# Attention stage re-planned: keys' maxima two pairs ahead, v copies shared with GpSimd, gate logits copied on VectorE, slots' rows scaled per head on ScalarE

## The chip, the cores and the metric

One core of one Trainium2 chip. The metric is the time of one execution in device microseconds; lower is better. The engines are named as in the profile: PE (TensorE matmul), PEld (its weight loads), DVE (VectorE), ACT (ScalarE), POOL (GpSimd) and SP (SyncE, which here only issues DMAs).

## What is computed

Three layers follow one another: attention without a sequence-by-sequence matrix, a top-1 mixture of experts, and a product of two projections.

```python
def _attn_ref(q, k, v):                      # 8 batches, 8 heads, 576 positions, 64 channels
    q_s = np.exp(q - np.max(q, axis=-1, keepdims=True)); q_s /= q_s.sum(-1, keepdims=True) + 1e-09
    k_s = np.exp(k - np.max(k, axis=2, keepdims=True));  k_s /= k_s.sum(2, keepdims=True) + 1e-09
    kv = np.einsum('bhsd,bhse->bhde', k_s, v)
    return np.einsum('bhsd,bhde->bhse', q_s, kv)
def _moe_ref(x, modality_id, w_gate, modality_bias, w1, w2):   # 4608 tokens, 8 experts, F = 1024
    logits = x @ w_gate + modality_bias[modality_id]
    e_idx = np.argmax(logits, axis=1)
    gate_w = softmax(logits)[arange, e_idx]
    for e in range(E):
        out[mask] = gate_w[mask] * (np.maximum(x[mask] @ w1[e], 0.0) @ w2[e])
def _moe2_ref(x, w1, w2, w3, w_out):
    return ((x @ w1) * (x @ w2)) @ w3 @ w_out
```

The keys' softmax runs over the positions, so its maximum is taken per channel over all 576 of them; the queries' softmax runs over the 64 channels of each head.

## The kernel before, in words

**Attention.** Two batches make a pair, so there are four pairs, c = 0 to 3. All large tiles exist twice (`z = c % 2`): `kt`, `qt`, `vt`. For each pair, `load` brings k, q and v in two DMAs each. `keys(c)` takes the maximum over positions: a tree of four `tensor_tensor` on DVE for each half of the heads (L303 to L306), four PE transposes into a PSUM bank (L312), a reduction on DVE (L315), eight small matmuls that spread the maxima over the partitions again (L320), a copy to `kr` on ACT (L323); then, for each of four groups g of two heads, three subtractions (L329, on DVE for c = 0, on GpSimd for the others) and one exponential on ACT (L330). `kvs(c)` copies v into `vp`, beside a column of ones (L341, ACT), multiplies (L348, PE), divides into `bd` on DVE (L355 to L357) and adds columns of gate logits to `bd` (L361 to L372), so that one product later gives the attention output, its sum and the gate logits. `queries(n)`, twelve of them, take three of a pair's nine position blocks each: maximum (L383) and subtraction (L384) on DVE into one of two tiles `qs`. `attend(c, j)`, nine per pair, transposes a block (L400, banks 6 and 7 in turn), takes exponentials on ACT (L403), multiplies by `bd` (L413) and copies the logits (L421) and the output (L422) from PSUM on ACT.

**Routing.** `route(c)` turns a pair's logits into expert, rank and gate. After the first two pairs (`BEARLY` = 4 batches) `early_table` and `early_lists` (L559 to L634) choose three expert slots of 512 tokens that can already be filled, with a final selection matmul on PE (L626, `pick`). The tile `ord` that comes of it holds the tokens' numbers and gates.

**Expert slots.** `slot(P, n)`: n = 0 to 2 are the early ones, six wide and one narrow slot follow. For each slot the rows of x are gathered by GpSimd's indirect DMA (L730, four tiles of 128 tokens), scaled on DVE by gate and sum (L736 to L738), transposed (L754), split into high and low parts on ACT and DVE (L758, L759), as are the weights (L701, L703), multiplied by w1 (L779), passed through ReLU and split (L765, L766), multiplied by w2 (L801) and copied out (L804). The experts' SBUF region lies over the attention's tiles: the first write there (`"Mb"`) waits until the last attend is over.

**Order.** Nothing is issued in the order of the text. Each step is added to a `Plan` with an engine, a cost, and what it reads and writes; `Plan.order` plays the steps through with these costs and puts on each engine the ready step with the lowest priority number (its number in the text plus `pri`). The engines then run that order in sequence, and each waits on semaphores for what it reads. So a changed cost or priority moves instructions on all engines. The first Plan covers attention, routing, slots 0 to 2 and the start of the next; a second one follows a branch (L927).

**The rest** (from about 600 us): the projections' weights are combined, then two stages of matrix products whose time is PE's.

Of the kernel before, what the change touches and what calls it, by code (L numbers as in the profile page):

```python
# [6 lines left out]
F32 = mybir.dt.float32  # L7
# [32 lines left out]
class Plan:  # L40
# [5 lines left out]
    def __init__(self, lat=0.12):  # L46
        self.lat = lat
        self.steps, self.last, self.readers = [], {}, {}

    def add(self, eng, cost, fn, r=(), w=(), pri=0.0, slack=0.0):  # L50
        i = len(self.steps)
        deps = set()
        for k in r:
            if k in self.last:
                deps.add(self.last[k])
            self.readers.setdefault(k, []).append(i)
        for k in w:
# [86 lines left out]
def body(tc, q, k, v, mod, wgate, mbias, w1, w2, m1, m2, w3, wo, out):  # L144
    nc = tc.nc
    V, G, SC, PE, SP = nc.vector, nc.gpsimd, nc.scalar, nc.tensor, nc.sync
    P = Plan()
    ctx = ExitStack()
# [145 lines left out]
    def keys(c):  # L294
# [26 lines left out]

        P.add("P", 1.8, to_rows, r=[K("cm", z)], w=[K("bk", 5)])
        P.add("S", ps_(512), lambda: SC.copy(r_.rearrange("p h d -> p (h d)"), bk), r=[K("bk", 5)], w=[K("kr", z)])  # L323
        for g in range(4):
            hs = slice(2 * g, 2 * g + 2)
            kg = [K("k", z, g)]
            en, e_, c_ = ("G", G, gt_(1152)) if c else ("V", V, vt_(1152))
            for js in (slice(3 * i, 3 * i + 3) for i in range(3)):
                P.add(en, c_ / 3 + 0.05, lambda hs=hs, e_=e_, js=js: e_.tensor_tensor(k_[:, hs, js], k_[:, hs, js], r_[:, hs].unsqueeze(2).to_broadcast([128, 2, 3, D]), op=ALU.subtract), r=[K("kr", z)], w=kg)  # L329
            P.add("S", sb_(1152), lambda hs=hs: SC.activation(k_[:, hs], k_[:, hs], AF.Exp), w=kg)  # L330

    def kvs(c):
# [6 lines left out]
        for g in range(4):  # L339
            w_ = vp[g % 2]  # L340
            P.add("S", sb_(1152), lambda g=g, w_=w_: SC.copy(w_[:, :, :, 0:64], v_[:, 2 * g : 2 * g + 2]), r=[K("v", z, g)], w=[K("vp", g % 2)])  # L341

            def mm(g=g, w_=w_):
                for j in range(NT):
                    for y in range(2):
                        for a in range(2):
                            p_ = slice(64 * y, 64 * y + 64)
                            PE.matmul(kv(y)[64 * a : 64 * a + 64, g], lhsT=k_[p_, 2 * g + a, j], rhs=w_[p_, a, j], start=(j == 0), stop=(j == NT - 1))  # L348

            P.add("P", 1.4, mm, r=[K("k", z, g), K("vp", g % 2)], w=[K("bk", 4), K("bk", 5)])  # L350
        for y in range(2):
# [18 lines left out]

            P.add("P", 0.9, gates, r=[K("kT", y), "wg"], w=[K("bk", 4 + y)])
            P.add("S", 0.2, lambda bk=bk, b_=b_: SC.copy(b_[:, :, 65:73], bk[:, 0:32].rearrange("p (c e) -> p c e", c=4)), r=[K("bk", 4 + y)], w=[K("bdg", n)])  # L372

    def queries(n):
# [6 lines left out]
        kq = [K("q", z, g) for g in range(4)]  # L381
        js = slice(3 * g, 3 * g + 3)
        P.add("V", vt_(1536), lambda: V.tensor_reduce(x[:, :, js], q_[:, :, js], axis=AX.X, op=ALU.max), r=kq, w=[K("qx", z, g)])  # L383
        P.add("V", vt_(1536), lambda: V.tensor_tensor(qs[(3 * c + g) % 2].rearrange("p j h d -> p h j d"), q_[:, :, js], x[:, :, js].unsqueeze(3).to_broadcast([128, H, 3, D]), op=ALU.subtract), r=kq + [K("qx", z, g)], w=[K("qs", (3 * c + g) % 2)])  # L384

    scattered, kept = [False], []

    def attend(c, j):
# [43 lines left out]

# [255 lines left out]
    def slot(P, n, after=(), parts="lsab", T=None, again=False):  # L688
# [16 lines left out]
        if "l" in parts:  # L705
# [26 lines left out]
            P.add("D", 5.9, lambda: wload("w2r", w2, "o (k p) f -> p (o k) f"), r=[rk_, "Ma"] + ([K("landed", xk) for _, _, xk in tiles] if n == 0 else []), w=[K("w2r", i) for i in range(8)], slack=2.0)  # L732
            for t, x_, xk in tiles:
                heads = x_.rearrange("p (h e) -> p h e", e=65)
                sums = heads[:, :, 64]
                P.add("V", 0.1, lambda sums=sums: V.tensor_scalar(sums, sums, 1e-9, None, op0=ALU.add), w=[xk], pri=-230)  # L736
                P.add("V", 0.12, lambda sums=sums: V.reciprocal(sums, sums), w=[xk], pri=-230)
                P.add("V", vt_(512), lambda t=t, heads=heads, x_=x_: V.scalar_tensor_tensor(out=x_[:, 0:512].rearrange("p (h e) -> p h e", e=64), in0=heads[:, :, 0:64], scalar=o[:, t, 1:2].bitcast(F32), in1=heads[:, :, 64:65].to_broadcast([128, H, D]), op0=ALU.mult, op1=ALU.mult), r=[ok], w=[xk], pri=-230)  # L738

# [582 lines left out]
```

## Time and profile before

| | us |
|---|---|
| median of 3 runs | 1216.51 (1213.94 to 1218.99) |
| profiled execution: time | 1220.7 |
| profiled execution: span from first to last instruction | 1219.0 |
| PE busy in the span | 1133.9 (93%) |
| DVE busy | 875.9 (72%) |
| ACT busy | 514.4 (42%) |
| POOL busy | 547.4 (45%) |

The span is what the views cut up; the 1.7 us between it and the execution's time lie around it. Times in the rows are us from the start of the span.

### The profile page before, as it was taken

The page shows a single profiled execution, that of the slowest core. Times are in us where ns is not written, and L with a number is a line of the kernel's source. Part 1 is how long each engine was busy: PE and PEld are TensorE (multiplying, and loading weights), DVE is VectorE, ACT ScalarE, POOL GpSimd, SP SyncE. Part 2 cuts the span into 40 slices and gives each one's busy share as a digit, 9 for nine tenths or more (in the row PEclk, how much of TensorE's full clock was granted, in tenths as well). Part 3 has the DMA queues.
Part 4 walks back from the last instruction along what each step waited for, and adds up shares of the span by engine and source line. Part 5 has one row for each costly group of instructions (what it writes and reads, how often), then busy time and mean ns, then how long its engine had stood idle before and what let it go on. Part 6 is the DMA issues. An engine that isn't in the chain of part 4 may idle for free.

```text
span 1219.0 us, 22861 instructions
## 1 busy us (share of the span) xinstructions
PE 1133.9 (93%) x8605; PEld 1033.1 (85%) x8605; DVE 875.9 (72%) x1483; ACT 514.4 (42%) x965; POOL 547.4 (45%) x536
## 2 busy tenths in 40 slices
PE   3677799899989999999999999999999999999996
PEld 3566677677878888888988999999999999999996
DVE  7878588888769989888645757576666689765550
ACT  3557564233334334334544332424242445655550
POOL 0355357843234344323133455555645576443332
PEclk9878789989999999999999999999999999999998
DMA  9982555654347566455644334444443348977741
GB/s 356 391 331 82 206 146 157 129 195 145 129 111 265 163 202 216 144 186 181 222 167 140 101 110 137 117 130 118 118 141 107 107 131 262 341 256 235 235 140 50
DMA packets 156139, 216.29 MB, mean 177 GB/s; under 512 B 19791, under 2 KB 90995, under 8 KB 156019
## 3 DMA queue, kind: packets, MB, share of 16 engines
q1 hardware_dynamic: 148946, 195.15, 49.9%
q0 software_dynamic: 7072, 19.60, 5.1%
q8 instruction: 69, 1.13, 0.4%
q14 instruction: 52, 0.42, 0.1%
HBM read 156.51 MB, written 74.97 MB: 190 GB/s over the span
## 4 chain that ended last, share of the span: by engine, by line
PE 68%; DVE 1%; DMA 1%; issue 1%; POOL 0%; ACT 0%; SPq 0%; DVEq 0%; POOLq 0%; ACTq 0%
PE pb L1134 29%; PE pb L1267 13%; PE pb L801 12%; PE pb L779 10%; PE pb L1025 3%; PE pb L754 1%; DMA ca<-p_dram 1%; PE pb L1012 1%; DMA p_dram<-ca 0%; DVE ar L1059 0%; DVE ar L999 0%; DVE ar L703 0%; POOL out_dram L1241 0%; DVE ca L1110 0%; SPq L1230 0%
## 5 line engine op out<-in xcount | busy, mean ns | idle before, releaser
L1134 PE MATMUL pb<-al,ar 128*128 128x384 f32 x1728 | 307.7, 335 | 1.1 <-ACT sx L1140 0.8
L1134 PEld LDWEIGHTS pb<-al,ar 128*128 128x128 f32 x1728 | 300.0, 188 | 1.6 <-ACT sx L1140 1.1
L801 PE MATMUL pb<-ar 128*128 128x512 f32 (+1 forms) x960 | 217.7, 385 | 0.0
L779 PE MATMUL pb<-ar 128*128 128x512 f32 (+1 forms) x960 | 216.0, 386 | 0.0
L779 PEld LDWEIGHTS pb<-ar 128*128 128x128 f32 x960 | 176.7, 192 | 35.2 <-DVE ar L759 0.4
L801 PEld LDWEIGHTS pb<-ar 128*128 128x128 f32 x960 | 175.2, 191 | 33.6
L1267 PE MATMUL pb<-ar 128*128 128x256 f32 x1512 | 182.9, 283 | 2.2 <-issue 1.3
L1267 PEld LDWEIGHTS pb<-ar 128*128 128x128 f32 x1512 | 181.8, 192 | 3.2 <-issue 1.3
L999 DVE TENSOR_TENSOR ar<-ca,ar 128x512 fp32r<-128x512 f32 x140 | 106.8, 770 | 55.2 <-ACT ar L998 43.7
L831 POOL TENSOR_TENSOR ca<-ca 128x512 f32<-128x512 f32 x40 | 57.3, 1437 | 107.4 <-DVE ca L830 98.4
L998 ACT CAST ar<-ca 128x512 fp32r<-128x512 f32 x140 | 86.2, 622 | 44.8 <-DMA ca<-p_dram 13.6
L765 ACT ACTIVATE ar<-pb 128x512 fp32r<-128x512 f32 (+1 forms) x80 | 46.1, 578 | 135.4 <-PE pb L779 118.2
L1140 ACT COPY sx<-pb 128x384 f32<-128x384 f32 x96 | 45.9, 481 | 90.8 <-PE pb L1134 60.9
L329 POOL TENSOR_TENSOR kt<-kt,kr 128x384 f32<-128x384 f32 x36 | 49.5, 1409 | 67.2 <-ACT kr L323 63.6
L1168 POOL TENSOR_TENSOR ca<-ca 128x384 f32<-128x384 f32 x48 | 54.1, 1128 | 52.1 <-DVE ca L1168 52.1
L804 ACT COPY yo<-pb 128x512 f32<-128x512 f32 (+1 forms) x40 | 22.6, 566 | 119.2 <-PE pb L801 115.3
L766 DVE SCALAR_TENSOR_TENSOR ar<-pb,ar 128x512 fp32r<-128x512 f32 (+1 forms) x80 | 52.4, 656 | 26.4 <-ACT ar L765 23.4
L703 DVE TENSOR_TENSOR ar<-w2r,ar 128x512 fp32r<-128x512 f32 x60 | 49.7, 862 | 21.2 <-ACT ar L701 20.6
L1143 POOL TENSOR_TENSOR ca<-ca,sx 128x384 f32<-128x384 f32 x24 | 29.4, 1224 | 77.7 <-ACT sx L1140 77.5
L1140 ACT COPY ca<-pb 128x384 f32<-128x384 f32 x48 | 22.9, 480 | 86.2 <-PE pb L1134 83.1
L1134 PE MATMUL pb<-thm,ar 128*128 128x384 f32 x288 | 58.2, 336 | 0.0
L730 POOL DMA_INDIRECT ca<-x_dram,ord x38 | 40.0, 1053 | 39.5 <-issue 13.0
(282 smaller groups left out, 1777.3 us busy)
## 6 DMA issues: line engine op xcount, KB each, us to landing
p_dram<-ca SPq DMA_DIRECT2D x168, 192.0 KB
ca<-p_dram SPq DMA_DIRECT2D x126, 256.0 KB
w1r<-in_moe_w_dram SPq DMA_DIRECT2D x10, 2048.0 KB
w2r<-in_moe_w_dram SPq DMA_DIRECT2D x10, 2048.0 KB
ca<-in_moe_w_dram SPq DMA_DIRECT2D x32, 512.0 KB
kt<-in_k_dram SPq DMA_DIRECT2D x8, 1152.0 KB
qt<-in_q_dram SPq DMA_DIRECT2D x8, 1152.0 KB
vt<-in_v_dram SPq DMA_DIRECT2D x8, 1152.0 KB
```

The lines of the kernel that those rows point to most:

```text
L329: P.add(en, c_ / 3 + 0.05, lambda hs=hs, e_=e_, js=js: e_.tensor_tensor(k_[:, hs, js], k_[:, hs, js], r_[:, hs].unsqueeze(2).to_broadcast( ...
L703: P.add(g, c, lambda: e.tensor_tensor(lo(), raw(), hi().bitcast(F32), op=ALU.subtract), r=[K(nm + "r", i), K(nm + "h", i), extra], w=[K(nm ...
L766: P.add("V", vt_(N), lambda hh=hh, hl=hl, p=p: V.scalar_tensor_tensor(out=hl(), in0=p(), scalar=0.0, in1=hh().bitcast(F32), op0=ALU.max, o ...
L779: PE.matmul(p(), lhsT=W1(i)[:, TURN[kk], ms], rhs=XT(z)[:, kk, cols], start=(kk == 0 and c == 0), stop=(kk == 3 and c == 2))
L801: PE.matmul(p(), lhsT=W2(i)[:, f, ns], rhs=HT(y)[:, f, cols], start=(f == 0 and c == 0), stop=(f == 7 and c == 2))
L831: P.add("G", gt_(512), lambda: G.tensor_tensor(Tf, Tf, Qf, op=ALU.add), r=[K("Q", b)], w=[K("T", b)])
L998: P.add("S", (ps_ if psum else sb_)(n), lambda: SC.copy(hi(), src), r=sk, w=[hk], pri=pri)
L999: P.add("V", vt_(n), lambda: V.tensor_tensor(lo(), src, hi().bitcast(F32), op=ALU.subtract), r=list(sk) + [hk], w=[lk], pri=pri)
L1134: PE.matmul(bk(j), lhsT=Mt[:, f, a, i, m, t], rhs=X(y, x)[:, t], start=(fresh and t == 0 and n == 0), stop=(t == 1 and n == 2), skip_group ...
L1140: P.add("S", ps_(HB), lambda j=j, to=to: SC.copy(S(to), bk(j)), r=[bkk(j)], w=[sk(to)])
L1168: P.add(eng, c(HB), lambda: e.tensor_tensor(t[:, sl], x, y, op=op), r=kk, w=[k_])
L1267: PE.matmul(bk(j), lhsT=At[z][:, m, i, f], rhs=Bt[:, x, y, f], start=(fresh and f == 0 and n == 0), stop=(f == 3 and n == 2), skip_group_c ...
```

## The change

It does these things:

- `keys(c)` is added two pairs ahead (`keys(1)` before the loop, `keys(c + 2)` after attend 8 of pair c), and uses the transposes' banks 7 and 6 in turn, where it used bank 5, which `kvs` uses too.
- Pair 0's subtractions go from DVE to GpSimd; of pair 1's twelve, four go from GpSimd to DVE (`SUBS_V`). Of the sixteen v copies, eight go to GpSimd (`VP`).
- The gate logits of each attend are copied from PSUM by DVE (`L2V`).
- Every kind of step gets a shift of its priority (`RANK`), several costs change, and the first Plan assumes 0.20 us between engines, not 0.12.
- From slot 1 on, sums and reciprocals are taken for two tiles at once, multiplied by the gate on DVE, and each head's 64 columns are scaled by an activation of their own on ACT, eight to a tile, where one DVE instruction did a tile.

```diff
+RANK = dict(load=-15, tree=-60, subs=-150, exps=15, kv=60, tail=-15, vp=-250, q=100, row=100)
+AFTER = (8, 8, 8)
+SUBS_V = (0, 1, 0, 0)
+VP = ("GSSG", "GSGG", "SSGG", "SSGS")
+L2V = 1
...
-    P = Plan()
+    P = Plan(0.2)
...
-        bk = bank[5]
+        qb = (7, 6)[rot("qb", 2)]
+        bk, bkk = bank[qb], K("bk", qb)
...
-            en, e_, c_ = ("G", G, gt_(1152)) if c else ("V", V, vt_(1152))
-            for js in (slice(3 * i, 3 * i + 3) for i in range(3)):
+            for i in range(3):
+                en, e_, c_ = ("V", V, 0.55) if i < SUBS_V[c] else ("G", G, 1.3)
+                js = slice(3 * i, 3 * i + 3)
...
-            P.add("S", sb_(1152), lambda g=g, w_=w_: SC.copy(w_[:, :, :, 0:64], v_[:, 2 * g : 2 * g + 2]), r=[K("v", z, g)], w=[K("vp", g % 2)])
+            P.shift = RANK["vp"]
+            en = VP[c][g]
+            e_, c_ = dict(S=(SC.copy, sb_(1152)), G=(G.tensor_copy, 1.35))[en]
...
-        P.add("S", 0.28, lambda: SC.copy(l_, pv[:, :, :, 64:73]), r=pk, w=[lk])
+        en, e_, c_ = ("V", V.tensor_copy, 0.2) if L2V else ("S", SC.copy, 0.28)
+        P.add(en, c_, lambda: e_(l_, pv[:, :, :, 64:73]), r=pk, w=[lk])
...
+                    if n == 0:
+                        P.add("V", vt_(512), lambda rows=rows, to=to, gate=gate: V.scalar_tensor_tensor(out=to, in0=rows[:, :, 0:D], scalar=gate, in1=rows[:, :, D : D + 1].to_broadcast([128, H, D]), op0=ALU.mult, op1=ALU.mult), r=[ok], w=[two[t]], pri=pri)
+                        continue
+                    P.add("V", 0.15, lambda rows=rows, gate=gate: V.tensor_scalar(rows[:, :, D], rows[:, :, D], gate, None, op0=ALU.mult), r=[ok], w=[two[t]], pri=pri)
+                    def scale(rows=rows, to=to):
+                        for i in range(H):
+                            SC.activation(to[:, i], rows[:, i, 0:D], AF.Copy, scale=rows[:, i, D : D + 1])
+                    P.add("S", 1.6, scale, w=[two[t]], pri=pri)
...
     kvs(0)
+    keys(1)
     biases()
     for c in range(4):
         load("k", c + 2)
-        keys(c + 1)
...
             attend(c, j)
+            if c < 2 and j == AFTER[c]:
+                keys(c + 2)
```

**On GpSimd**, all of the attention stage. `kt0` holds the keys of pairs 0 and 2, `kt1` those of pairs 1 and 3; before, one row stands for each of pairs 1, 2 and 3:

```order
L329 TENSOR_TENSOR kt1_116<-kt1_116,kr1_143 128x2x192 x12
L329 TENSOR_TENSOR kt0_115<-kt0_115,kr0_142 128x2x192 x12
L601 IOTA qt0_128 128x128
L329 TENSOR_TENSOR kt1_116<-kt1_116,kr1_143 128x2x192 x12
L730 DMA ca_94<-x_dram_59,ord_93 128x520 x5
```

and now (L341 are the subtractions, L358 the copies of v):

```order
L341 TENSOR_TENSOR kt0_115<-kt0_115,kr0_142 128x2x192 x7
L358 COPY vp1_139<-vt0_117 128x18x64
L341 TENSOR_TENSOR kt0_115<-kt0_115,kr0_142 128x2x192 x3
L341 TENSOR_TENSOR kt1_116<-kt1_116,kr1_143 128x2x192 x5
L358 COPY vp0_138<-vt1_118 128x18x64
L341 TENSOR_TENSOR kt1_116<-kt1_116,kr1_143 128x2x192 x3
L358 COPY vp0_138<-vt1_118 128x18x64
L358 COPY vp1_139<-vt1_118 128x18x64
L341 TENSOR_TENSOR kt0_115<-kt0_115,kr0_142 128x2x192 x12
L358 COPY vp0_138<-vt0_117 128x18x64
L341 TENSOR_TENSOR kt1_116<-kt1_116,kr1_143 128x2x192 x12
L756 DMA ca_94<-x_dram_59,ord_93 128x520 x4
```

Pair 0's twelve subtractions now stand first, eight of pair 1's follow, and the copies stand between them.

**On PE**, round the maxima of pair 3's keys (`mx1`, `cm1`) before. `bd0` and `bd1` at this place are pair 2's:

```order
L361 MATMUL pb4_75<-ident_84,bd0_150 64x128 x4
L361 MATMUL pb5_76<-ident_84,bd1_151 64x128 x4
L369 MATMUL pb4_75<-wg_156,kTs0_154 64x8 x8
L369 MATMUL pb5_76<-wg_156,kTs1_155 64x8 x8
L400 MATMUL pb7_78<-ident_84,qs1_133 128x128 x4
L312 MATMUL pb5_76<-ident_84,mx1_141 128x128 x4
...
L320 MATMUL pb5_76<-ident_84,cm1_145 64x128 x8
```

and now, where L365 with `kt0` is pair 2's kv product:

```order
L322 MATMUL pb6_77<-ident_84,mx1_141 128x128 x4
...
L365 MATMUL pb4_75<-vp0_138,kt0_115 64x65 x2
...
L330 MATMUL pb6_77<-ident_84,cm1_145 64x128 x8
...
L380 MATMUL pb4_75<-ident_84,bd0_150 64x128 x4
L380 MATMUL pb5_76<-ident_84,bd1_151 64x128 x4
```

Pair 3's maxima stood behind pair 2's finished kv product and its tail; they now stand inside that product.

**On ACT**, round the rows of slot 1 before (L758 splits a transposed block, L804 copies a result of slot 0 out):

```order
L701 CAST ar_2224<-w1r_1407 128x512 x3
L758 CAST ar_2224<-pb5_76 128x2x256
L804 COPY yo_2229<-pb3_2220 128x512
L758 CAST ar_2224<-pb7_78 128x2x256
```

and now:

```order
L776 ACTIVATE ca_94<-ca_94 128x64 x16
L844 COPY yo_2229<-pb3_2220 128x512
L798 CAST ar_2220<-pb5_76 128x2x256
L798 CAST ar_2220<-pb7_78 128x2x256
```

Sixteen activations, for two tiles of 128 tokens, stand ahead of the copy of slot 0's first result.

## Rows read from the trace of the kernel before

**Rows 1.** By stretch: busy PE, PEld, DVE, ACT, POOL; granted clock, DMA share, GB/s.

```profile
0.00:141.00 141.00, 90.61 (x2428) 77.92 (x2432) 110.47 (x193) 77.92 (x139) 52.12 (x52) 0.85 0.71 264
...
52.00:68.10 16.10, 7.01 (x186) 6.09 (x188) 16.03 (x17) 7.87 (x10) 16.10 (x12) 0.75 1.04 396
...
141.00:161.00 20.00, 15.28 (x324) 12.15 (x320) 7.29 (x19) 12.16 (x29) 4.91 (x5) 0.78 0.95 347
```

**Rows 2.** PE's waits from 0 to 161 us: total, times, longest.

```profile
PE pb L348 <- ACT kt L330: 24.9, 7, 5.1
```

**Rows 3.** Instructions in order of time, the chain of pair 3: start, duration.

```profile
114.04 15.98 POOL L329 TENSOR_TENSOR kt<-kt,kr 128x384 f32<-128x384 f32 x11
...
129.09 2.22 ACT L330 ACTIVATE kt<-kt 128x1152 f32<-128x1152 f32 x2 [3.15 <-POOL kt L329]
...
140.21 0.57 PEld L626 LDWEIGHTS <-qt 128*128 128x128 bf16 x18
...
161.02 14.23 PE L779 MATMUL pb<-ar 128*128 128x512 f32 x51
```

**Rows 4.** DVE's waits from 0 to 141 us: total, times, longest.

```profile
DVE rk L355 <- PE pb L348: 8.1, 4, 3.8
...
DVE ltri L249 <- POOL ltf L248: 2.1, 1, 2.1
DVE qx L383 <- DMA qt<-in_q_dram: 1.8, 1, 1.8
```

**Rows 5.** DVE's groups by line and shape, 0 to 141 us: busy, mean ns, idle before.

```profile
L384 DVE TENSOR_TENSOR qs<-qt,qx 128x1536 f32<-128x1536 f32 x12 | 22.5, 1879 | 5.2 <-PE pb L400 5.2
...
L303 DVE TENSOR_TENSOR tr<-kt 128x1024 f32<-128x1024 f32 x8 | 12.1, 1518 | 2.9 <-DMA kt<-in_k_dram 2.7
...
L329 DVE TENSOR_TENSOR kt<-kt,kr 128x384 f32<-128x384 f32 x12 | 5.7, 551 | 0.0
L621 DVE TENSOR_TENSOR qt<-qt 128x384 bf16<-128x384 f32 x6 | 5.4, 899 | 0.0
...
L569 DVE SCALAR_TENSOR_TENSOR t_tak<-t_tar,t_jE 128x3 f32<-128x3 f32 x1 | 1.0, 958 | 0.0
...
L470 DVE TENSOR_TENSOR ca<-pb,cnt 128x72 f32<-128x72 f32 x2 | 0.5, 225 | 0.0
```

**Rows 6.** Single DVE instructions in order of time, free of and beside GpSimd's work.

```profile
6.32 1.22 DVE L303 TENSOR_TENSOR tr<-kt 128x1024 f32<-128x1024 f32 x1 [2.71 <-DMA kt<-in_k_dram]
...
17.10 5.71 DVE L329 TENSOR_TENSOR kt<-kt,kr 128x384 f32<-128x384 f32 x12
...
22.73 1.75 DVE L384 TENSOR_TENSOR qs<-qt,qx 128x1536 f32<-128x1536 f32 x1
...
60.86 2.56 DVE L384 TENSOR_TENSOR qs<-qt,qx 128x1536 f32<-128x1536 f32 x1
```

**Rows 7.** GpSimd's groups by line and shape, 0 to 160 us, columns as in rows 5.

```profile
L329 POOL TENSOR_TENSOR kt<-kt,kr 128x384 f32<-128x384 f32 x36 | 49.5, 1409 | 67.2 <-ACT kr L323 63.6 <-PE pp L413 3.6
...
L261 POOL MEMSET zer<- 128x584 int32 x1 | 0.6, 611 | 0.0
```

**Rows 8.** GpSimd's subtractions of pair 1 alone: ns min/median/max, first and last start.

```profile
L329 POOL TENSOR_TENSOR kt<-kt,kr x12: 988/1182/2504, 51.8 to 66.1; 128x384 f32<-128x384 f32 x12
```

**Rows 9.** PE's waits from 160 to 330 us.

```profile
PE pb L465 <- DVE cnt L471: 4.6, 1, 4.6
...
PE pb L754 <- DVE ca L738: 1.9, 2, 1.4
```

**Rows 10.** One group of DVE from 161 to 345 us, columns as in rows 5.

```profile
L738 DVE SCALAR_TENSOR_TENSOR ca<-ca,ord 128x512 f32<-128x512 f32 x16 | 13.4, 836 | 0.0
```

**Rows 11.** ACT's groups by line and shape, 160 to 600 us, columns as in rows 5.

```profile
L701 ACT CAST ar<-w2r 128x512 fp32r<-128x512 f32 x80 | 49.2, 622 | 2.9
...
L457 ACT ACTIVATE ca<-ca 128x72 f32<-128x72 f32 x2 | 0.5, 264 | 2.9 <-DVE ca L456 2.9
```

**Rows 12.** One product of a wide slot in order of time.

```profile
317.46 21.92 PE L779 MATMUL pb<-ar 128*128 128x512 f32 x96
```

More of the change, by code (lines that the diff above doesn't have):

```diff
@@ L47, in __init__ @@
         self.lat = lat
-        self.steps, self.last, self.readers = [], {}, {}
+        self.steps, self.last, self.readers, self.shift = [], {}, {}, 0.0
     def add(self, eng, cost, fn, r=(), w=(), pri=0.0, slack=0.0):
@@ L63, in add @@
         deps.discard(i)
-        self.steps.append((eng, cost, fn, sorted(deps), i + pri, slack))
+        self.steps.append((eng, cost, fn, sorted(deps), i + pri + self.shift, slack))
     def order(self):
@@ L272, in load @@
             fn = lambda dst=dst, i=i: SP.dma_start(dst, src[2 * c + i].rearrange("(g y) (r j) d -> (y r) g (j d)", y=2, j=NT))
-            P.add("D", 3.7, fn, w=[K(n, z, g) for g in (2 * i, 2 * i + 1)], slack=1.0)
+            P.add("D", 3.05, fn, w=[K(n, z, g) for g in (2 * i, 2 * i + 1)], slack=1.0)
+        P.shift = 0.0
     def smalls():
@@ L300, in keys @@
         t2 = tr4[:, :, 0:2].rearrange("p h j d -> p h (j d)")
+        P.shift = RANK["tree"]
         for i in range(2):
@@ L312, in over_partitions @@
                 PE.transpose(bk[:, 128 * i : 128 * i + 128], xf[:, 128 * i : 128 * i + 128], ident)
-        P.add("P", 0.9, over_partitions, r=[K("mx", z)], w=[K("bk", 5)])
-        P.add("V", vt_(512), lambda: V.tensor_reduce(x_, bk.rearrange("p (c t) -> p c t", c=8), axis=AX.X, op=ALU.max), r=[K("bk", 5)], w=[K("cm", z)])
+        P.add("P", 0.6, over_partitions, r=[K("mx", z)], w=[bkk])
+        P.add("V", vt_(512), lambda: V.tensor_reduce(x_, bk.rearrange("p (c t) -> p c t", c=8), axis=AX.X, op=ALU.max), r=[bkk], w=[K("cm", z)])
         def to_rows():
@@ L320, in to_rows @@
                     PE.matmul(bk[64 * y : 64 * y + 64, 128 * i : 128 * i + 128], lhsT=x_[:, 2 * i + y : 2 * i + y + 1].to_broadcast([128, 64]), rhs=ident, start=True, stop=True)
-        P.add("P", 1.8, to_rows, r=[K("cm", z)], w=[K("bk", 5)])
-        P.add("S", ps_(512), lambda: SC.copy(r_.rearrange("p h d -> p (h d)"), bk), r=[K("bk", 5)], w=[K("kr", z)])
+        P.add("P", 0.75, to_rows, r=[K("cm", z)], w=[bkk])
+        P.add("S", ps_(512), lambda: SC.copy(r_.rearrange("p h d -> p (h d)"), bk), r=[bkk], w=[K("kr", z)])
         for g in range(4):
@@ L340, in kvs @@
             w_ = vp[g % 2]
[L341 removed]
+            P.shift = RANK["vp"]
+            en = VP[c][g]
+            e_, c_ = dict(S=(SC.copy, sb_(1152)), G=(G.tensor_copy, 1.35))[en]
+            P.add(en, c_, lambda g=g, w_=w_, e_=e_: e_(w_[:, :, :, 0:64], v_[:, 2 * g : 2 * g + 2]), r=[K("v", z, g)], w=[K("vp", g % 2)])
             def mm(g=g, w_=w_):
@@ L348, in mm @@
                             PE.matmul(kv(y)[64 * a : 64 * a + 64, g], lhsT=k_[p_, 2 * g + a, j], rhs=w_[p_, a, j], start=(j == 0), stop=(j == NT - 1))
-            P.add("P", 1.4, mm, r=[K("k", z, g), K("vp", g % 2)], w=[K("bk", 4), K("bk", 5)])
+            P.shift = RANK["kv"]
+            P.add("P", 1.1, mm, r=[K("k", z, g), K("vp", g % 2)], w=[K("bk", 4), K("bk", 5)])
+        P.shift = RANK["tail"]
         for y in range(2):
@@ L361, in tr @@
                     PE.transpose(bk[0:64, 128 * g : 128 * g + 128], b_[:, g, 0:64], ident)
-            P.add("P", 0.9, tr, r=[K("bd", n)], w=[K("bk", 4 + y)])
+            P.add("P", 0.7, tr, r=[K("bd", n)], w=[K("bk", 4 + y)])
             P.add("S", ps_(512), lambda bk=bk, T=T: SC.copy(T.rearrange("p c d -> p (c d)"), bk[0:64]), r=[K("bk", 4 + y)], w=[K("kT", y)])
@@ L369, in gates @@
                         PE.matmul(bk[64 * a : 64 * a + 64, 8 * g : 8 * g + 8], lhsT=T[:, g, 64 * a : 64 * a + 64], rhs=wg[:, 4 * (g % 2) + 2 * a + y], start=True, stop=True)
-            P.add("P", 0.9, gates, r=[K("kT", y), "wg"], w=[K("bk", 4 + y)])
+            P.add("P", 0.5, gates, r=[K("kT", y), "wg"], w=[K("bk", 4 + y)])
             P.add("S", 0.2, lambda bk=bk, b_=b_: SC.copy(b_[:, :, 65:73], bk[:, 0:32].rearrange("p (c e) -> p c e", c=4)), r=[K("bk", 4 + y)], w=[K("bdg", n)])
+        P.shift = 0.0
     def queries(n):
@@ L400, in tr @@
                 PE.transpose(pt[:, 128 * g : 128 * g + 128], q_[:, j % 3, 2 * g : 2 * g + 2].rearrange("p h d -> p (h d)"), ident)
-        P.add("P", 0.9, tr, r=[K("qs", y)], w=[K("bk", qb)])
+        P.shift = RANK["row"]
+        P.add("P", 0.65, tr, r=[K("qs", y)], w=[K("bk", qb)])
         P.add("S", ps_(512), lambda: SC.activation(T, pt, AF.Exp), r=[K("bk", qb)], w=[K("qT", n)])
@@ L413, in mm @@
                             PE.matmul(px[64 * i : 64 * i + 64, a, o : o + 73], lhsT=T[p_, t0 : t0 + 64], rhs=bd[2 * z + y][p_, 2 * i + g], start=True, stop=True)
-        P.add("P", 0.8, mm, r=[K("qT", n)] + [K(x_, 2 * z + y) for x_ in ("bd", "bdg") for y in range(2)], w=pk)
+        P.add("P", 0.65, mm, r=[K("qT", n)] + [K(x_, 2 * z + y) for x_ in ("bd", "bdg") for y in range(2)], w=pk)
         xb = (j // 2 + 5 * c) % 5
@@ L430, in attend @@
                 store()
+        P.shift = 0.0
     def scatter(dst, src):
@@ L732, in slot @@
             P.add("D", 5.9, lambda: wload("w2r", w2, "o (k p) f -> p (o k) f"), r=[rk_, "Ma"] + ([K("landed", xk) for _, _, xk in tiles] if n == 0 else []), w=[K("w2r", i) for i in range(8)], slack=2.0)
[L733 to L738, printed above, removed]
+            for h in hs:
+                wide = xg[h].rearrange("p t (g e) -> p t g e", e=D + 1)
+                two, pri = [K("xg", h, t) for t in range(2)], -230
+                for group in (((0,), (1,)) if n == 0 else ((0, 1),)):
+                    sums, kk = wide[:, group[0] : group[-1] + 1, :, D], [two[t] for t in group]
+                    P.add("V", 0.15, lambda sums=sums: V.tensor_scalar(sums, sums, 1e-9, None, op0=ALU.add), w=kk, pri=pri)
+                    P.add("V", 0.17, lambda sums=sums: V.reciprocal(sums, sums), w=kk, pri=pri)
+                for t in range(2):
+                    gate = o[:, 2 * (h if len(hs) == 2 else 0) + t, 1:2].bitcast(F32)
+                    rows, to = wide[:, t], xg[h][:, t, 0 : H * D].rearrange("p (g e) -> p g e", e=D)
+                    if n == 0:
[6 more added lines that the diff above has]
+                    P.add("S", 1.6, scale, w=[two[t]], pri=pri)
```

12 lines of the change are left out of this document (10 added, 2 removed).

## The prediction

> **What bounds the kernel now.** I read the table by stretch first, then the waits of PE and DVE, then the instructions in order of time. Behind 343 us PE has next to no gap to give: the slots' product is one unbroken run of 96 matmuls in 21.92 us, 0.228 each [rows 12]. What can move lies in front of that. The first expert matmul starts at 161.0 [rows 3], and until 141 PE is busy for 90.6 of 141 us at a granted clock of 0.85 of the upper level [rows 1]. Its largest wait there is the kv product's, on the keys' exponentials: 24.9 us in seven pieces [rows 2]. The exponentials wait for GpSimd. Pair 3 shows the chain: its subtractions run from 114 to 130, its last exponentials start at 129.1, and the selection matmul, which stands behind pair 3's kv tail, starts at 140.2 [rows 3]. From there to the first expert matmul it is 20.8 us: pair 3's nine attends, the gather, and the release of the attention's memory. So I call the selection's start T, 140.2 now, and ask where it goes.
>
> The reader should also see that DVE is not idle in this: 110.5 of 141 us busy [rows 1], and in 52 to 68 us, while GpSimd subtracts, both are busy all the time.
>
> **Part one: keys two pairs ahead.** Before, GpSimd does three blocks of twelve subtractions with gaps of some 15 us, 49.5 us busy in all [rows 7]. Now it does 44 (12, 8, 12, 12) and eight copies. At 49.5 / 36 = 1.375 each the subtractions are 60.5 us. No row shows a copy of 1152 elements on GpSimd. The nearest from below is the memset, 0.611 / 584 = 1.05 ns an element, so 1.2 us; from above the two-input subtraction at 1.375 / 384 = 3.6 ns, so 4.1. I take 1.5, near the memset, since a copy too has no second input: 12 us, bounds 10 to 33. So GpSimd has 72.5 us of work from 17 on, where pair 0's subtractions began on DVE [rows 6]: without a gap 90. It will have gaps, because PE meets pair 3's transposes only inside pair 2's kv product. I place pair 3's last subtraction at about 112, against 130. Its exponential and its kv tail add what they did (130 to 140.2): by this chain T is no earlier than about 113 and rather 122.
>
> **Part two: DVE's own work up to T.** This replaces GpSimd's chain as the one that ends last, as I reckon.
> Busy until 141: 110.5 [rows 1]. Off: twelve subtractions, 5.7 [rows 5]. On: four of pair 1, 4 x 5.7 / 12 = 1.9. On: the logits' copies. Of 36, 27 stand before T in DVE's new order; the nearest row is another PSUM read of 72 columns, 0.225 us [rows 5], so 6.1. Off: two query subtractions that now stand behind T, 3.5. Sum 109.3.
> In that sum are waits for GpSimd that show as long durations: a tree's first step takes 1.22 alone and 1.52 in the mean, a query subtraction 1.75 alone, 2.56 beside GpSimd's work and 1.88 in the mean [rows 5, 6]; a table step of three columns took 0.96 [rows 5]. I take 0.3 x 8 for L303, 2.0 for the tree's other steps, 1.6 for L384, 7 for nine such table steps, 2 for the six of L621 (0.90 in the mean, where I allow a third of it for waits), 3 for routing: 18. That leaves 91 of plain work.
> The new waits: 53 DVE instructions with two SBUF inputs stand between GpSimd's first subtraction and the early table (24 of the trees, 10 of queries, 12 of routing, 7 more). GpSimd is busy for 72.5 of the 95 us from 17 to 112, 0.76. A subtraction alone takes 0.99 [rows 8], so whoever finds one running waits half of it, 0.5: 53 x 0.76 x 0.5 = 20. Bounds: 0.13 (L384's mean less 1.75) and 0.81 (2.56 less 1.75), so 5 to 33. The table's steps fall behind GpSimd's last subtraction and are short.
> Unavoidable waits at the start, for constants and the first k and q: 2.1 + 2.7 + 1.8 = 6.6 [rows 4, 6]. The 8.1 us behind the kv product [rows 4] mostly go, as kv is ready earlier; I leave 7 for these, other PE results and the gaps between instructions. T = 91 + 20 + 6.6 + 7 = 125. Bounds: 113 (GpSimd's chain) and 140 (33 for waits, 9 more idle). Gain on T: 15.
>
> The Trainium skill (SBUF — State Buffer, section "SBUF: two separate sides") says that a DVE instruction with two SBUF inputs and a GpSimd instruction exclude each other for the whole instruction. The trace agrees: the subtraction takes 0.99 to 2.50 us [rows 8] and DVE's stretch as well [rows 6]. By that rule alone the two queues of work would be added and not overlapped, 44 x 0.99 + 12 on GpSimd and some 42 on DVE, 98 us from 17 on (the 42 are the plain durations of the 53 instructions and of L621): T = 115 at best, which forbids no more than my lower bound does.
>
> **Part three: T to the first expert matmul.** Nine attends, the gather and the x transposes are the same steps; 20.8 us, with PE's clock granted at 0.78 in that stretch and DMA at 0.95 [rows 1]. The logits' copies leave ACT here, and DVE has little else. The weights' DMAs wait for the early table, which in DVE's new order ends just ahead of T, so they fall on the gather: I add 1 us, bounds 0 to 5.
>
> **Part four: the slots' rows on ACT.** 8 wide slots of 32 activations and a narrow one of 16 make 272. Nearest row: ACT on 72 columns of SBUF, 0.264 [rows 11], so 72 us in all, spread over some 440 us; half of that, if they overlap, is the lower bound. ACT is busy for 42% of the whole span. It is hidden by the matmuls as long as ACT reaches each PSUM eviction in time: one falls due every 12 matmuls (2.7 us), three banks turn. DVE is freed of 0.84 us a tile [rows 10]. PE waited 4.6 us for DVE's count in front of the second ranks matmul (L465) and 1.9 for scaled rows [rows 9]. I take 2 off the first (0 to 4.6) and add 1 to the second: two tiles took 1.7 on DVE, sixteen activations take 2.1 to 4.2. Net gain 1.
>
> **Sum.** 15 - 1 + 1 = 15. The profiled execution took 1220.7 (span 1219.0 and 1.7 around it), 0.35% above the median of 1216.5; it would take 1205.7, and the median 1216.5 - 15 = **1201.5**.
>
> **Rivals.**
> - *GpSimd's chain is the last, DVE keeps up.* For it: the chain alone gives 113, and PE's 24.9 us of waits is what the change aims at. Against: DVE was full in 52 to 68 us. T = 113, and the 4.6 of L465 goes: 27 - 1 + 4.6 = 30.6, 1186. Chance 0.17.
> - *DVE and GpSimd slow each other down.* Subtractions that were on DVE, 0.48 each, and copies that were on ACT are now where they hold DVE up. T = 136 to 140, no gain in the slots: 0 to 3 us gained, 1214 to 1217. Chance 0.14.
> - *The keys don't get ahead*, because k's buffer comes free only with kv two pairs back and DMA is full (share 1.04 in 52 to 68 us [rows 1]): pair 3 starts as now, and only the slots' 1 us is gained, 1215. Against: the third pair's loads are in by the time that the second's subtractions end. Chance 0.04.
> - *Slower: ACT holds PE up in the slots.* Sixteen activations are 4.2 us in one piece. With four casts beside them (0.6 each [rows 11]) ACT is away for 6.6 us; from 4.9 on (two banks' 5.5 less an eviction's 0.6) PE stops. 1.7 us for each of 17 half slots would be 29, less the 15: 1230. Against: activations of 64 columns may well overlap, and the new order puts casts and activations of one slot mostly on either side of an eviction. Chance 0.08.
>
> **How the numbers follow.** Forecast 0.57, with T from 118 to 133: 1194 to 1209. What a measurement can tell from no change is 0.5%, 6 us. Faster by more: 0.57 + 0.17 = 0.74. Within: 0.14 + 0.04 = 0.18. Slower: 0.08. The range has to reach over the gainless rivals and part of the larger gain: 1189 to 1215 leaves out the slower case and about half of the 1186 case.
>
> **What would show it.** In the profile of the changed kernel: the selection matmul (L652) at about 125 and the first expert matmul at 147; GpSimd with one gap or two and its last subtraction near 112; DVE busy for over 85% of 17 to 125; PE's wait for exponentials (24.9) halved; query subtractions longer than 1.88 in the mean; PE in the slots without new waits for ACT, the run of 96 matmuls still at 21.9. I am wrong if T stays above 136, if L358 on GpSimd takes 3 us or more, or if PE waits for L776 slot by slot.

## The result, and the profile after

The changed kernel takes 1230.54 us (median of 4 runs, 1228.24 to 1232.45) against 1215.22 for the kernel before on the same chip: a ratio of 1.0122, 95% interval 1.0086 to 1.0159. It is slower by 1.2%, 29 us above the forecast of 1201.5 and outside its range. The profiled spans are 1230.7 and 1219.0.

The table by stretch of the changed kernel, columns as in [rows 1]:

```profile
0.00:141.00 141.00, 84.72 (x2351) 73.49 (x2351) 109.39 (x208) 64.54 (x97) 67.78 (x68) 0.88 0.70 255
...
161.00:343.00 182.00, 166.47 (x726) 132.62 (x725) 141.05 (x313) 106.77 (x248) 100.27 (x115) 0.95 0.54 149
343.00:600.00 257.00, 250.53 (x1132) 206.37 (x1131) 207.19 (x335) 144.67 (x319) 89.79 (x68) 0.99 0.54 174
```

DVE is busy for 109.39 of 141 us, as reckoned (109.3), but PE has done less by 141 than before (84.7 against 90.6), and in the third row, where nothing was to give, PE now idles for 6.5 of 257 us. The instructions in order of time, from the attention to the first expert matmul; they answer to [rows 3]:

```profile
53.36 2.23 PE L436 MATMUL pp<-bd,qT 64*64 64x73 f32 x64
...
62.50 0.68 PE L365 MATMUL pb<-vp,kt 64*64 64x65 f32 x27 [4.22 <-issue]
...
70.19 0.42 DVE L315 TENSOR_TENSOR mx<-mx,kt 128x256 f32<-128x256 f32 x1
...
74.10 0.93 PE L365 MATMUL pb<-vp,kt 64*64 64x65 f32 x24 [3.84 <-issue]
...
76.89 0.66 PE L322 MATMUL pb<-ident,mx 128*128 128x128 f32 x4
...
80.20 13.67 POOL L341 TENSOR_TENSOR kt<-kt,kr 128x384 f32<-128x384 f32 x12 [15.73 <-ACT kr L333]
...
110.80 13.59 POOL L341 TENSOR_TENSOR kt<-kt,kr 128x384 f32<-128x384 f32 x12 [7.09 <-ACT kr L333]
...
137.08 1.03 PE L365 MATMUL pb<-vp,kt 64*64 64x65 f32 x52 [1.74 <-issue]
...
144.24 0.68 PE L652 MATMUL pb<-qt 128*128 128x60 bf16 x18
...
162.52 12.66 PE L819 MATMUL pb<-ar 128*128 128x512 f32 x48
```

The first attend product starts at 53.4 (before at 35.6), pair 2's subtractions at 80.2 (before 83.1), pair 3's at 110.8 (before 113.1), the selection at 144.2 (before 140.2) and the first expert matmul at 162.5 (before 161.0). So 1.5 us of the 11.7 between the spans are lost by then, and 10.2 behind it. PE's waits from 0 to 161 us (total, times, longest), which answer to [rows 2]:

```profile
PE pb L322 <- DVE mx L315: 16.1, 3, 9.3
PE pb L365 <- issue: 10.2, 4, 4.2
PE pp L436 <- ACT qT L426: 7.6, 4, 6.6
PE pb L422 <- DVE qs L405: 5.6, 1, 5.6
PE pp L436 <- issue: 5.2, 3, 2.6
PE pb L380 <- DVE bd L376: 4.9, 1, 4.9
...
PE pb L365 <- ACT kt L343: 0.7, 1, 0.7
```

The wait that the change aims at fell from 24.9 to 0.7, and the whole of PE's waits rose: added up over all rows of this view, those for ACT went from 32.9 to 14.7 us, those for DVE from 15.1 to 30.9, and "issue", in which PE waits for nothing that the profile shows, from 6.9 to 15.4. That is the reading of the front: the stall did not go, it moved.

In the slots, the same view from 161 to 620 us; these five rows are all (22.8 us; before 14.5):

```profile
PE pb L819 <- DVE ar L806: 10.7, 3, 4.6
PE pb L794 <- ACT ca L776: 8.5, 12, 2.5
PE pb L794 <- DVE ar L799: 1.8, 2, 1.4
PE pb L491 <- ACT yo L844: 1.0, 1, 1.0
PE pb L794 <- PEq L969: 0.8, 1, 0.8
```

The first row names DVE, but it is ACT that is late. One such place in order of time:

```profile
375.56 11.73 ACT L776 ACTIVATE ca<-ca 128x64 f32<-128x64 f32 x32 [1.49 <-issue]
...
381.62 2.31 PE L819 MATMUL pb<-ar 128*128 128x512 f32 x9
...
387.20 1.55 ACT L805 ACTIVATE ar<-pb 128x512 fp32r<-128x512 f32 x3
...
387.81 1.29 DVE L806 SCALAR_TENSOR_TENSOR ar<-pb,ar 128x512 fp32r<-128x512 f32 x2 [5.16 <-ACT ar L805]
...
388.55 16.55 PE L819 MATMUL pb<-ar 128*128 128x512 f32 x60 [4.62 <-DVE ar L806]
```

ACT scales the rows of a whole slot, 32 activations, in one piece of 11.73 us. The evictions (L805) stand behind it; PE fills its three banks and stops for 4.62 us. The stop comes with a second loss: still in it, from 387.4 us, TensorE's granted clock is at the lower of its two levels until 394.2, and the 60 matmuls of the last line take 16.55 us, where at 0.228 each [rows 12] they would take 13.7. The group of those activations from 161 to 620 us (busy, mean ns, idle before):

```profile
L776 ACT ACTIVATE ca<-ca 128x64 f32<-128x64 f32 x272 | 93.0, 348 | 26.1 <-DVE ca L772 16.9 <-issue 1.5
```

And three groups of the attention, from 0 to 161 us:

```profile
L341 POOL TENSOR_TENSOR kt<-kt,kr 128x384 f32<-128x384 f32 x44 | 55.1, 1286 | 39.4 <-ACT kr L333 39.4
...
L405 DVE TENSOR_TENSOR qs<-qt,qx 128x1536 f32<-128x1536 f32 x12 | 25.4, 2120 | 5.6 <-PE pb L422 5.5
...
L358 POOL COPY vp<-vt 128x1152 f32<-128x1152 f32 x8 | 10.4, 1302 | 23.8 <-PE pb L365 18.2 <-issue 5.5
```

### The profile page after: what moved, and what is told of

Same layout as the page of the kernel before. It is cut to its first block, busy times and chain, and to the rows that moved or that the text cites. A ratio compares the mean times of both kernels' runs of the same rounds, so it can differ in the third digit from the quotient of the medians.

```text
span 1230.7 us, 23061 instructions
## 1 busy us (share of the span) xinstructions
PE 1133.1 (92%) x8605; PEld 1029.1 (84%) x8605; DVE 865.2 (70%) x1477; ACT 588.3 (48%) x1193; POOL 559.7 (45%) x552
## 4 chain that ended last, share of the span: by engine, by line
PE 65%; issue 1%; DVE 1%; ACT 1%; DMA 1%; POOL 1%; SPq 0%; DVEq 0%; POOLq 0%; ACTq 0%
PE pb L1176 26%; PE pb L1309 13%; PE pb L841 12%; PE pb L819 9%; PE pb L1067 4%; ACT ca L776 1%; PE pb L794 1%; DMA ca<-p_dram 1%; DVE ar L1041 1%; PE pb L1054 1%; POOL ca L1210 0%; DVE ca L1210 0%; DMA p_dram<-ca 0%; SPq L1272 0%; POOL out_dram L1283 0%
## 5 line engine op out<-in xcount | busy, mean ns | idle before, releaser
L776 ACT ACTIVATE ca<-ca 128x64 f32<-128x64 f32 x272 | 93.0, 348 | 26.1 <-DVE ca L772 16.9
L805 ACT ACTIVATE ar<-pb 128x512 fp32r<-128x512 f32 (+1 forms) x80 | 45.5, 577 | 94.9 <-PE pb L819 89.3
L1182 ACT COPY sx<-pb 128x384 f32<-128x384 f32 x96 | 46.1, 483 | 90.4 <-PE pb L1176 57.6
L1210 POOL TENSOR_TENSOR ca<-ca 128x384 f32<-128x384 f32 x48 | 53.4, 1113 | 45.6 <-DVE ca L1210 45.6
L341 POOL TENSOR_TENSOR kt<-kt,kr 128x384 f32<-128x384 f32 x44 | 55.1, 1286 | 39.4 <-ACT kr L333 39.4
L729 POOL TENSOR_TENSOR ar<-w2r,ar 128x512 fp32r<-128x512 f32 x20 | 29.2, 1464 | 77.5 <-ACT ar L727 77.4
## 6 DMA issues: line engine op xcount, KB each, us to landing
qt<-in_q_dram SPq DMA_DIRECT2D x8, 1152.0 KB, 10.2
```

Source lines behind the costliest of these rows:

```text
L341: P.add(en, c_, lambda hs=hs, e_=e_, js=js: e_.tensor_tensor(k_[:, hs, js], k_[:, hs, js], r_[:, hs].unsqueeze(2).to_broadcast([128, 2, 3, ...
L729: P.add(g, c, lambda: e.tensor_tensor(lo(), raw(), hi().bitcast(F32), op=ALU.subtract), r=[K(nm + "r", i), K(nm + "h", i), extra], w=[K(nm ...
L776: SC.activation(to[:, i], rows[:, i, 0:D], AF.Copy, scale=rows[:, i, D : D + 1])
L1182: P.add("S", ps_(HB), lambda j=j, to=to: SC.copy(S(to), bk(j)), r=[bkk(j)], w=[sk(to)])
L1210: P.add(eng, c(HB), lambda: e.tensor_tensor(t[:, sl], x, y, op=op), r=kk, w=[k_])
```

## The experiments

Theory S: the rows on ACT cost the time, by pieces that stand in front of evictions. Its rival: the loss is made in front and only shows in the slots. For the front, theory F (pair 0's subtractions on GpSimd start everything late), theory K (the keys' chain does set the selection) and rival W (other chains and PE's code set it). Ratios below are against the kernel before on the same chip, with their interval.

**e1, slots' rows back on DVE.** The block that adds L772 and L776 is replaced by the old one:

```
...
-  P.add("S", 1.6, scale, w=[two[t]], pri=pri)
...
+  P.add("V", vt_(512), ... V.scalar_tensor_tensor(out=x_[:, 0:512]..., op0=ALU.mult, op1=ALU.mult), ...)
```

> The changed kernel with the slots' rows scaled on DVE as before, all else as changed. Theory S (ACT's pieces of 16 and 32 activations hold up the PSUM evictions and PE waits: 20.2 us of PE's waits behind ACT from 161 to 620, against 10.9 behind DVE before): 9 to 11 us come back, 1220 us, and the lag behind the kernel before stays at 1 to 3 us from the first expert matmul to the end. Rival (the loss is the front's lateness and TensorE's clock, and ACT's waits are only where it shows): 1227 to 1231.

1210.82 us, 0.9946 (0.9927 to 0.9964): faster than before. Against the change's 1.0122 that is 1.8%, some 21 us, twice what theory S asked for. The first expert matmul starts at 162.97, so nothing of it comes from the front; PE's waits from 161 to 620 us are 10.4 us and none is for ACT. PE, busy 166.5 us in the first of these stretches with the rows on ACT, is now busy for 174.0. So PE's waits, 22.8 us in the change, account for 12.4 of the 21. The granted clock accounts for some more: it is 0.95 and 0.99 in the two stretches of the change and 0.97 and 1.00 here, by these shares 182 x 0.02 + 257 x 0.01 = 6 us, an estimate.

```profile
161.00:343.00 182.00, 174.04 (x794) 142.90 (x795) 154.32 (x344) 74.81 (x136) 101.79 (x116) 0.97 0.52 150
343.00:600.00 257.00, 256.28 (x1228) 215.01 (x1227) 218.66 (x365) 106.25 (x190) 93.47 (x69) 1.00 0.61 195
```

**e2, the rows on ACT alone,** in the kernel before. 

> The kernel before with nothing but the slots' rows scaled on ACT. Theory S: 8 to 12 us slower than before, 1224 to 1228, with the first expert matmul at 161 as before and a wait of 4 us or more for evictions where 32 activations stand in one piece. Rival (rows on ACT only hurt in the changed order of steps): within 3 us of before.

1235.49 us, 1.0136 (1.0098 to 1.0173), some 17 us, more than the 8 to 12 expected. PE's waits from 161 to 620 us rise from 14.5 to 24.4. With e1 this shows from both sides that the rows on ACT cost the time, though not all of it as waits. The same stall ends here at 391 us:

```profile
391.19 15.50 PE L793 MATMUL pb<-ar 128*128 128x512 f32 x60 [4.61 <-DVE ar L780]
```

**e5, each activation a step of its own.**

```
...
-  P.add("S", 1.6, scale, w=[two[t]], pri=pri)
+  for i in range(H):
+      P.add("S", 0.36, ... SC.activation(to[:, i], rows[:, i, 0:D], ...), w=[two[t]], pri=pri)
```

> The changed kernel with each of the 272 activations planned as a step of its own of 0.36 us instead of eight in one of 1.6. If the piece is what hurts (evictions cannot come between): PE's waits behind ACT in the slots fall from 20 to under 8 us, 1217 to 1222. If ACT's sum of 93 us is what hurts: no change, 1228 to 1232.

1217.18 us, 0.9991 (0.9970 to 1.0012): some 16 of the 21 us come back, and PE's waits from 161 to 620 us are 11.4. Up to 368 us ACT's pieces are still of 16 and 32 activations, but shorter; behind that they are of 1 to 14. So the run joins two things, shorter pieces and split ones, and doesn't tell what each is worth. One whole piece and the stop behind it:

```profile
360.40 7.77 ACT L775 ACTIVATE ca<-ca 128x64 f32<-128x64 f32 x32 [1.49 <-issue]
...
370.57 16.49 PE L816 MATMUL pb<-ar 128*128 128x512 f32 x60 [3.77 <-DVE ar L803]
```

32 take 7.77 us, 0.243 each, where the change takes 11.73, 0.367 each. Heads are moved up within their row (65 columns apart to 64), so each activation writes where its forerunner read. In the change's trace 238 of them wait for ACT's own count and start 0.381 us behind their forerunner (median); the 17 that open another tile within a piece wait for DVE's count instead and start 0.255 behind it. So the wait for the one before is what spreads them. As single steps the planner can take the two tiles in turn, and what an activation waits for would be two back and done; they start 0.239 apart (median). That reason is argued: the trace doesn't say which count each waits for.

The Trainium skill (ScalarE: Activation LUTs, section "What ACT_TABLE_LOAD costs") gives an activation 186 ns and 0.833 ns a column, 93 ns more for a pointer operand, and lets neighbours overlap by 93 ns. By that page 64 columns with one pointer would take 332 ns and follow one another every 239, an estimate. e5 agrees (337 in the mean, 0.243 us apart); the change, at 0.367, doesn't get the overlap.

**e6, the step priced at 2.8 in the planner** instead of 1.6. 

> The changed kernel with the step of eight activations priced at 2.8 us in the planner instead of 1.6 (the trace has 8 x 0.348). If the wrong price made the planner put four steps in a row ahead of an eviction: PE's waits behind ACT in the slots fall below 10 us of 20 and the time to 1215 to 1222. If a step of 2.8 us is too long as such, or the place is set by the rows' arrival: 1227 to 1232.

1230.49 us, 1.0095 (1.0074 to 1.0116): no better. Four steps still stand in a row (in order of time), and PE's longest wait for the evictions is now 6.6 us. The wrong price alone is not the cause.

```profile
368.75 11.75 ACT L776 ACTIVATE ca<-ca 128x64 f32<-128x64 f32 x32 [1.49 <-issue]
```

**e3, pair 0's subtractions on DVE:** `SUBS_V = (3, 1, 0, 0)`. 

> The changed kernel with pair 0's twelve key subtractions on DVE as before. Theory F (the front loses at its start: the first attend starts at 53.4 instead of 35.6 because GpSimd subtracts pair 0's keys beside DVE): the first attend starts at 36 to 40, the selection matmul at 128 to 134 instead of 144.2, 10 to 15 us faster than changed, 1216 to 1221. Rival (the late start is made up for anyway, and later waits set the selection): selection matmul at 141 to 145, 1227 to 1231.

1231.45 us, 1.0099 (1.0059 to 1.0138). The first attend comes at 46.1, seven us earlier, and the selection at 139.8, but the first expert matmul only at 161.5. Pair 2's subtractions start no earlier than in the change (80.20):

```profile
81.17 15.17 POOL L341 TENSOR_TENSOR kt<-kt,kr 128x384 f32<-128x384 f32 x12 [17.18 <-ACT kr L333]
```

Theory F falls as the cause of the slower time: the late start is real, and nearly all of it is made up for anyway.

**e7 and e10: the logits back on ACT (`L2V = 0`), then the v copies too,** both with e1's rows. 

> As e1 (rows of the slots on DVE), and the gate logits copied on ACT as before. Theory L (the copies on DVE hold up ACT's own copy of the same product, ca L446 <- DVE ca L445 5.8 us, and through it PE's next product, 4.2 us in one piece at 122): the selection matmul comes 4 us or more before e1's 141.2, and the time is 3 to 6 us below e1's 1210.8. Rival (those waits are covered, PE's code transfers and the work itself fill the time): selection at 139 to 143, time within 3 us of e1.

> As e7 with the v copies on ACT too: of the change only the keys two pairs ahead, the ranks and the planner's number are left. If the keys' placement can move the selection at all, it does so here, where GpSimd and DVE are unburdened: selection at 125 to 135 and 1196 to 1206. Rival (the selection is tied to the work of PE and ACT up to it, not to the keys): selection at 137 to 143, 1207 to 1213.

e7: 1218.42 us, 0.9978 (0.9961 to 0.9995), selection at 144.3. e10: 1218.98 us, 0.9980 (0.9963 to 0.9997), selection at 144.2 and first expert matmul at 168.3 (its profiled execution took 1225.25, 6 us above the median). Neither helps; both are some 0.3% slower than e1. So the copies were no burden. e10 is not the keys' placement by itself, as I had put it: pair 0's subtractions are still on GpSimd, and the banks, costs and ranks of the change are in it too. It shows that the placement doesn't move the selection ahead in this company; alone it was not run.

**e11, e1 without the keys' subtractions, and e13, the kernel before without maxima and subtractions.** 

> As e1, without the 48 subtractions of the keys' maxima (part of the computation is left out; the exponentials still wait for the maxima). Theory K (GpSimd's subtractions and what they hold up on DVE set the selection): selection at or below 130, 1197 to 1203. Rival W (the attends' own chain through DVE, PE, ACT and PE's code transfers sets it): selection at 135 or later, 1205 to 1213.

> The kernel before without the keys' maxima and their subtractions (trees, transposes, rows and subtractions are left out; exponentials straight from the loads). It bounds what any placing of the keys can give. Theory K: PE's 24.9 us of waits for the exponentials go, selection at or below 122, 1195 to 1203. Rival W: they are replaced by waits for queries, evictions and code, selection at 130 or later, 1208 to 1216.

e11: 1201.91 us, 0.9854 (0.9837 to 0.9870), selection at 128.5 (e1: 141.2). e13: 1190.34 us, 0.9758 (0.9739 to 0.9776), selection at 119.7, first expert matmul at 141.2. Theory K holds in both: without the keys' work the selection comes 12.7 us earlier in e11 and 20.5 in e13. Both runs also take work off DVE (it is busy for 95.8 and 72.0 of the first 141 us, 111.9 in e1 and 110.5 in the kernel before), so they don't tell the chain from that load; and 20.5 us is what leaving the work out gives, a bound for any placing of it. What is next in line is seen in e13, in order of time:

```profile
46.25 0.51 PE L321 MATMUL pb<-vp,kt 64*64 64x65 f32 x19 [1.37 <-issue]
...
52.44 0.79 PE L321 MATMUL pb<-vp,kt 64*64 64x65 f32 x34 [3.28 <-issue]
...
58.68 1.51 PE L321 MATMUL pb<-vp,kt 64*64 64x65 f32 x87 [1.79 <-issue]
...
64.88 0.51 PE L342 MATMUL pb<-wg,kTs 64*64 64x8 f32 x11 [1.54 <-issue]
```

PE stops every 6.2 us, in the middle of a group of matmuls whose operands are there; all its "issue" from 0 to 161 us is 24.3.

**e12, that stop by itself:** 1400 matmuls of the kv product's shape in a row, no load running; then 1400 more beside twelve loads of 1152 KB. Nothing of the reference is computed. Each of these matmuls leaves two records in the trace, and the counts below are of records.

> The disputed cost by itself, nothing of the reference is computed: 1400 matmuls of 64x64 by 65 columns in a row without any load running, then 1400 more while twelve loads of 1152 KB run. If PE's 'issue' waits are code transfers that queue behind loads: no gap or gaps below 1 us in the first stretch, gaps of 2 us or more every 128 matmuls or so in the second, each ending 1 to 2 us behind the landing of a 16 KB transfer. If they are something else (the tile, the bank): both stretches alike.

In order of time:

```profile
1.45 7.72 PE L167 MATMUL acc<-a 64*64 64x65 f32 x351 [1.45 <-DVE a L159]
10.77 2.09 PE L167 MATMUL acc<-a 64*64 64x65 f32 x128 [1.60 <-issue]
14.77 2.09 PE L167 MATMUL acc<-a 64*64 64x65 f32 x128 [1.91 <-issue]
...
92.08 3.59 PE L167 MATMUL acc<-a 64*64 64x65 f32 x128 [4.93 <-issue]
98.28 3.35 PE L167 MATMUL acc<-a 64*64 64x65 f32 x128 [2.60 <-issue]
104.47 2.81 PE L167 MATMUL acc<-a 64*64 64x65 f32 x128 [2.85 <-issue]
```

And of the page's DMA queues (packets, MB, share) the one that carries code:

```profile
q8 instruction: 43, 0.70, 1.4%
```

After a first stock of 351 matmuls PE runs 128 and stops, again and again. The page of this run counts 11,248 matmuls and weight loads of PE and 43 transfers of instructions with 0.70 MB: 16 KB for each 128 matmuls with their weight loads. Without loads such a block comes every 3.5 to 4.0 us and PE waits 1.4 to 1.9 for it, more than I expected; beside the loads it comes every 6.2 us, at a lower granted clock (0.63 from 90 to 125 us). The landings tie the two together: each of the 40 stops of over 1 us ends 1.2 to 1.6 us after a 16 KB transfer of instructions has landed. In the change's trace the six "issue" waits of over 1 us, 15.0 of the 15.4 us, end 1.3 to 1.5 us after such a landing. "Issue" in the attention is PE waiting for its own code.

**e8, the kernel before with only the planner's hand-over time changed,** `P = Plan(0.2)` for 0.12, **and e9, e1 with 0.12.** 

> The kernel before with nothing changed but the planner's hand-over time, 0.12 to 0.2 us, which the change also sets. Theory P (e1's gain of 10 us in the slots, with the rows scaled as before, comes from the order that this number gives there: no 4.6 us wait of the ranks matmul, no 2.9 us wait for the transposed rows, and less time at the lower clock): 6 to 12 us faster than before, all of it behind the first expert matmul. Rival (the gain comes from what the changed attention leaves over for the slots): within 4 us of before.

> As e1, with the planner's hand-over time back at 0.12 us. Theory P: the slots' gain goes, 1217 to 1222. Rival: it stays, 1208 to 1213.

e8: 1208.76 us, 0.9896 (0.9878 to 0.9913), the fastest version here that leaves nothing out. e9: 0.9942 (0.9919 to 0.9965), as fast as e1. So one number, which I hadn't priced at all, is worth 1% in the kernel before, all of it in the slots (first expert matmul at 162.8, span 1204.0), and nothing in e1. PE's waits from 161 to 620 us fall from 14.5 to 8.1, among them that of the ranks matmul [rows 9] from 4.6 to 1.2, and from 161 to 343 us PE is busy for 176.3 us at a granted clock of 0.99, against 168.3 at 0.95; the clock is worth 182 x 0.04 = 7 us by this, an estimate. I read e1's gain over the kernel before in the same way, as another order in the slots with fewer waits (10.4) and less time at the lower clock; what in the order does it was not taken apart.

## Why the prediction was wrong

**What bounds the kernel: right as far as shown.** Without the keys' work T comes 12.7 to 20.5 us earlier (e11, e13), though chain and load on DVE were not told apart. The step from "the keys set it" to "the change brings them forward" was wrong.

**Part one, GpSimd's last subtraction at 112: failed.** It ended at 124.4. The prices were high, if anything: a subtraction took 1.286 us in the mean (1.375 reckoned), a copy 1.30 (1.5), 65.5 us in all against 72.5. What failed is "one gap or two": GpSimd waited 39.4 us for the maxima's rows and 23.8 in front of copies. DVE has pair 2's maxima at 70.6 us, but their transposes stand in PE's order behind pair 1's kv product, which has two waits for code of 4.2 and 3.8 us inside it; they start at 76.9, and the rows come at 79.5. That pair 0's subtractions now fall to GpSimd (first attend 18 us later) is not what makes them late: with these on DVE (e3) pair 2's subtractions start at 81.2. So "two pairs ahead" in the program gave 2.9 us for pair 2 and 2.3 for pair 3, little more than the rival that the keys don't get ahead allowed.

The end of this part failed too. From the last subtraction to T I took what it was, 10.2 us; it was 19.8 (124.4 to 144.2). Pair 3's kv product stands there in four pieces, between pair 2's attends and behind the last v copies, with waits for code of 1.0 and 1.7 us. So the 5.6 us that GpSimd was earlier than before were lost again, and 4 more; what part of this is PE's order and what the code was not tried.

**Part two, T = 125: failed by 19 us.** DVE's busy time was right, its waits were not: I left 6.6 + 7 us idle until T, and it was idle for 31.6 of 141 us; from 17 to 125 us it was busy for 82%, where over 85 was my sign. DVE's own work was not what ends last. L405 rose to 2.12 us in the mean, as said, and a logits' copy took 0.284 (0.225 reckoned). Among the rivals, those without a gain in T came nearest, but T is later than either had it, and not by their mechanisms alone: PE's waits for DVE and for code took the place of those for the exponentials. My sum had no term for "issue"; 6.9 us of it stood in the trace of before. How much T would gain without PE's waits for code was not tried. Of my signs for being wrong, T above 136 came true, PE's wait for L776 in part (12 times, 8.5 us), and the copy of 3 us did not.

**Part three, 21.8 us from T to the first expert matmul:** 18.3, in the change's favour.

**Part four, a net gain of 1: failed, and it alone takes the time out of the range** (without it, e1: 1210.8). It cost some 21 us in the change and 17 by itself. The price was taken from an activation that stands alone (0.264), sixteen at 2.1 to 4.2 us; in a row each takes 0.367, since it waits for the one before, and sixteen 5.92. And I held that the order puts pieces on either side of an eviction; the trace has 32 in one piece twice (11.75 us at 312.5, 11.73 at 375.6), where 4.9 was the limit that I worked out myself. The rival "ACT holds PE up in the slots" described this at 1230, with a chance of 0.08: its mechanism was right, its place was not (two stalls of 4.6 us, each behind a piece of 32, and many small ones, and not 17 of 1.7), and that it met my total is partly luck, since the 15 us on T were not there.

**What I left out.** The planner's number in the diff had no term in the sum; in the kernel before it is worth 12.7 us (e8), in e1 nothing (e9). Nor had the time at the lower clock that stands behind a stop of PE.

## What to carry to other kernels

Before a wait is priced as a gain, look for what is next in PE's own queue: here the removed 24.9 us came back as waits for DVE and for code. Work moved to an engine that is idle on average still has to fit between that engine's deadlines, so price the longest piece that an order can make, with each instruction's wait for its forerunner, and not the sum. A stop of PE can cost more than its length, as the granted clock showed here. In a kernel ordered by a planner, run each of its numbers alone: a hand-over time moved from 0.12 to 0.2 was worth as much as the whole change, with the other sign.

## What the runs showed of the hardware

Short matmuls outran PE's supply of code. 128 matmul records of 65 columns with their weight loads take 2.09 us, and their 16 KB of instructions come every 3.5 to 4.0 us, every 6.2 beside loads that move some 390 GB/s (e12). Each stop ended 1.2 to 1.6 us after such a transfer had landed. The slots' matmuls last longer, and 96 of them take 21.9 us without a stop [rows 12]. In the attention the stops show as "issue" inside a group.

A small activation that waits for ACT's own previous one started 0.381 us behind it, one that waits for DVE's count 0.255 (the change, 64 columns); in e5 they followed every 0.24.

Near the end of a stop of 4.6 us TensorE's granted clock fell to its lower level for 6.8 us, and the 60 matmuls that followed took 16.55 us for 13.7 (the change, 387 to 405 us).
